# First batch in float32 through PV: probabilities scaled in place and turned by TensorE's one-pass float32 transpose

## The chip, the cores and the metric

The kernel runs on one core of one Trainium2 chip. The metric is device time in microseconds (us) of one execution; lower is better. Three runs of the kernel before gave 605.25, 607.4 and 608.04 us, median 607.4.

## What is computed

Causal attention over 4 batches, 12 heads, 448 positions and head size 64, and behind it a dense gated layer over all 1792 rows. The weights arrive as 64-bit floats.

```python
scores = (1.0 / np.sqrt(64)) * np.matmul(q, k.transpose(0, 1, 3, 2))
scores = np.where(mask, -1000000000.0, scores)          # mask: above the diagonal
scores = scores - np.max(scores, axis=-1, keepdims=True)
attn = np.exp(scores)
attn = attn / (np.sum(attn, axis=-1, keepdims=True) + 1e-09)
a = np.matmul(attn, v)                                  # [4, 12, 448, 64]
x = a.transpose(0, 2, 1, 3).reshape(1792, 768)
h = x @ w_in                                            # [768, 2048]
out = (h * (1.0 / (1.0 + np.exp(-1.702 * h)))) @ w_out  # [2048, 768]
```

## The kernel before

**Tiling.** The 448 positions of a batch are 7 chunks of 64. `cuts` makes two blocks of each batch: chunks 0 to 3 and chunks 4 to 6, so there are 8 blocks; n = 0 and n = 1 are batch 0. The 12 heads go in 6 pairs (u = 0 to 5, a "unit"); the two heads of a pair lie on the two halves of the 128 partitions. A chunk i looks at i + 1 chunks of keys, that is i // 2 + 1 tiles of 128 columns.

**Numbers.** Most products are float32 made of two float16 halves, high and low: `scaled` makes the high half (ScalarE or VectorE), `rest` the low half (VectorE), and three products (high-high, high-low, low-high) are added in PSUM. `halves` (L410) makes a product as two matmuls of 64 columns of the stationary operand. In batch 0 (`f32(b, u)`, L831) queries and keys stay float32 as they are: `turn` (L859) turns them by matmuls against an identity, and `scores32` multiplies in float32.

**A unit** (`unit`, L1174): scores into `ps_s`; `chunk` (L1079) subtracts the maximum and masks on VectorE (L1086) and takes the exponential on ScalarE (L1100), both in the float32 tiles `z`, of which there is one set for all units; GpSimd adds 1e-9 to the row sums (L1203); VectorE takes 1/sum (L1209). Then P = z/sum must be turned, so that the keys lie on the partitions. In block 0 (`pet=(0,)`) `p_turned` (L1129) builds a diagonal matrix of 1/sum (L1140, GpSimd or VectorE), multiplies z by it on TensorE in float32 into `ps_h`, and splits the result into `PT`, high and low. In all other blocks `p_pair` (L1112) splits z/sum into `p16`, high and low, and one DMA transpose (L1223) turns it into `PT`. `pv` (L1238) multiplies with V in three float16 products into `ps_v`, and every second unit splits the result into `xT`.

**V.** `v_batch` (L771) loads a whole batch's V into `vraw` in four loads, takes its largest norm (in batch 0 by the products of `gram` on TensorE, L610) and a scale from it; `v_pair` (L808) splits V for two units into `v16`.

**The dense layer.** `w_in_slice` (L633) loads, converts to float32 (`to_f32`: VectorE, and partly ScalarE) and splits one of 8 slices of w_in into `wib`; `w_out_load`, `w_out_scale` and `w_out_split` do the same for w_out, some of its raw data passing through `vraw`. `h_slice` (L1297) multiplies a block's `xT` with a slice into one of three `ps_h` buffers, and ScalarE and VectorE make the gate and the split `gT` from it; `out_tile` (L1350) multiplies with w_out and stores.

**Order.** Nothing runs by loop order: every step is given to `Ops.add` with its cost on each engine that may do it (the first named is preferred), its reads and writes, a priority and the time on the DMA engines. `Ops.order` tries 1500 orders on that model, with a model of TensorE's clock, and the best is issued: a fixed sequence for each engine's queue and for SP, which issues all DMAs.

## Time and profile before

| | |
|---|---|
| median of three runs | 607.4 us |
| profiled execution, its own time | 608.42 us |
| its span | 606.7 us |
| TensorE matmul (PE) busy | 567.6 us, 94% |
| VectorE (DVE) busy | 422.1 us, 70% |
| ScalarE (ACT) busy | 358.5 us, 59% |
| GpSimd (POOL) busy | 101.9 us, 17% |
| mean granted TensorE clock | 0.994 |

The span runs from the first to the last instruction. Busy shares are means over a kernel with different stages, so they are read by stretch of time. PEld is TensorE's loading of weights, which overlaps PE; SPq is SP's queue, which issues DMAs. A group of matmuls in the view in order of time carries about 0.2 us of modelled end, which the next group overlaps. "DMA" is the mean busy share of 16 DMA engines, "clock" the granted share of 2.4 GHz. In a row of a group, the numbers behind the bar are busy us, mean ns of one, and idle us before them with what ended it.

### The profile page before, as it was taken

Reading aid. Unit: us, or ns where it says so; the run is one execution under the profiler, and the core shown is the slowest. Engines: PE = TensorE matmul, PEld = TensorE weight load, DVE = VectorE, ACT = ScalarE, POOL = GpSimd, SP = SyncE. Lnnn points to the kernel's source line nnn. Section 1 sums busy time; section 2 is a strip of 40 time slices with the busy share of each in tenths; the row PEclk is TensorE's granted clock in tenths of the full one; section 3 lists DMA queues with packets and bytes.
Section 4 is the critical chain, followed back from the end, with each engine's and each line's share of the span. In section 5 each row is a group of like instructions: output and inputs, shape, how many; then the busy total and the mean of one; then the engine's idle time right before and its main releaser. Section 6 shows DMA issues by size and latency. Waiting matters only on the chain. (4 is left out here: it accounts for less than half of the span.)

```text
span 606.7 us, 22564 instructions
## 1 busy us (share of the span) xinstructions
PE 567.6 (94%) x9646; PEld 510.2 (84%) x9646; DVE 422.1 (70%) x1121; ACT 358.5 (59%) x826; POOL 101.9 (17%) x239
## 2 busy tenths in 40 slices
PE   4767798989999999999999999999999999999997
PEld 3555687876889899988988899998999999899986
DVE  3999999999978899977589869786686431202020
ACT  5779898998857767666566457675464321202120
POOL 2343330215410024110011223111000000000000
PEclk9999899999999999999999999999999999999999
DMA  8999579968688998998954998758662400000000
GB/s 278 228 311 296 178 230 315 237 141 149 123 178 162 162 165 144 166 168 163 171 99 85 167 176 144 144 99 139 96 122 58 90 14 16 1 28 3 28 27 28
DMA packets 217028, 83.84 MB, mean 138 GB/s; under 512 B 197728, under 2 KB 206688, under 8 KB 216928
## 3 DMA queue, kind: packets, MB, share of 16 engines
q1 hardware_dynamic: 216928, 82.40, 64.7%
q8 instruction: 75, 1.23, 0.8%
q14 instruction: 25, 0.20, 0.1%
HBM read 41.68 MB, written 5.51 MB: 78 GB/s over the span
## 5 line engine op out<-in xcount | busy, mean ns | idle before, releaser
L413 PE MATMUL ps_h<-xT,wib 128*64 128x192 f16 (+1 forms) x4608 | 247.1, 260 | 1.2 <-DVE gT L478 1.2
L1375 PE MATMUL ps_o<-wob,gT 128*64 128x384 f16 x2688 | 244.0, 326 | 1.6 <-DVE wob L478 1.4
L413 PEld LDWEIGHTS <-wib 128*64 128x64 f16 x4608 | 229.4, 110 | 7.2 <-issue 2.9
L1375 PEld LDWEIGHTS <-gT 128*64 128x64 f16 x2688 | 179.4, 110 | 31.9 <-issue 4.1
L1100 ACT ACTIVATE z<-z,cols 128x320 f32<-128x320 f32 (+6 forms) x168 | 84.0, 501 | 48.4 <-DVE cols L1086 47.3
L1337 DVE SCALAR_TENSOR_TENSOR ps_h<-t,ps_h 128x512 f32<-128x512 f32 (+1 forms) x64 | 40.1, 626 | 85.5 <-ACT t L1332 84.9
L1332 ACT ACTIVATE t<-ps_h,cols 128x512 f32<-128x512 f32 (+1 forms) x64 | 40.2, 629 | 73.6 <-PE ps_h L413 68.2
L478 DVE SCALAR_TENSOR_TENSOR p<-z,cols,p 128x384 f16<-128x384 f32 (+3 forms) x144 | 73.9, 541 | 3.3 <-ACT p L473 2.5
L1086 DVE CUSTOM_DVE_ANT_0 z<-ps_s,mask,cols 128x320 f32<-128x320 f32 (+6 forms) x126 | 56.7, 479 | 11.5 <-PE ps_s L1063 10.8
L1203 POOL TENSOR_SCALAR cols<-cols 128x2 f32<-128x2 f32 (+1 forms) x68 | 23.9, 352 | 195.4 <-ACT z L1100 184.1
L473 ACT ACTIVATE p<-z,cols 128x384 f16<-128x384 f32 (+3 forms) x82 | 44.6, 562 | 15.3 <-DVE cols L1209 8.2
L478 DVE SCALAR_TENSOR_TENSOR gT<-ps_h,gT 128x512 f16<-128x512 f32 (+1 forms) x64 | 39.4, 619 | 10.0 <-ACT gT L473 9.4
L1063 PE MATMUL ps_s<-kT,qT 128*64 128x64 f16 (+4 forms) x504 | 42.5, 273 | 1.8 <-DVE cols L1086 1.7
L1241 PE MATMUL ps_v<-PT,v 128*64 128x192 f16 (+3 forms) x864 | 41.3, 237 | 1.9 <-DVE xT L478 1.8
L1241 PEld LDWEIGHTS <-v 128*64 128x64 f16 x864 | 40.0, 110 | 3.6 <-issue 2.6
L473 ACT ACTIVATE gT<-ps_h 128x512 f16<-128x512 f32 (+1 forms) x54 | 29.4, 544 | 19.3 <-DVE ps_h L1337 19.0
L473 ACT ACTIVATE ob<-ps_o,cols 128x384 f32<-128x384 f32 x22 | 12.6, 573 | 37.6 <-PE ps_o L1375 37.6
L1100 ACT ACTIVATION_READ_ACCUMULATOR z<-z,cols 128x1 f32 x168 | 31.8, 189 | 0.0
L1063 PEld LDWEIGHTS <-qT 128*64 128x64 f16 x504 | 26.7, 110 | 5.5 <-issue 3.0
L1021 POOL TENSOR_SCALAR q<-q 128x512 f16<-128x512 f16 (+1 forms) x28 | 19.4, 694 | 54.5 <-ACT q L473 47.4
L475 DVE TENSOR_SCALAR p<-z,cols 128x256 f16<-128x256 f32 (+3 forms) x62 | 25.1, 423 | 3.7 <-DMA PT<-p 2.6
L473 ACT ACTIVATE wob<-wob 128x768 f32<-128x768 f32 (+1 forms) x20 | 22.1, 1104 | 7.7 <-DMA wob<-in_moe_w_in_dram 7.0
(95 smaller groups left out, 580.1 us busy)
## 6 DMA issues: line engine op xcount, KB each, us to landing
wob<-in_moe_w_in_dram SPq DMA_DIRECT2D x16, 768.0 KB, 6.9
wob<-in_moe_w_out_dram SPq DMA_DIRECT2D x9, 768.0 KB, 6.0
vraw<-in_moe_w_out_dram SPq DMA_DIRECT2D x7, 768.0 KB, 5.5
out_dram<-ob SPq DMA_DIRECT2D x28, 192.0 KB, 2.4
vraw<-in_v_dram SPq DMA_DIRECT2D x12, 384.0 KB, 5.1
kf<-in_k_dram SPq DMA_DIRECT2D x36, 112.0 KB, 3.5
qf<-in_q_dram SPq DMA_DIRECT2D x48, 64.0 KB, 2.8
qf<-in_q_dram SPq DMA_DIRECT2D x48, 48.0 KB, 2.8
```

Source lines behind the costliest of these rows:

```text
L413: nc.tensor.matmul(out[o : o + 64], lhsT[:, o : o + 64], rhs, start=start, stop=stop)
L473: nc.scalar.activation(out=dst, in_=src, func=AF.Copy, scale=sc)
L475: nc.vector.tensor_scalar(out=dst, in0=src, scalar1=sc, scalar2=None, op0=ALU.mult)
L478: nc.vector.scalar_tensor_tensor(out=dst, in0=src, scalar=sc, in1=hi, op0=ALU.mult, op1=ALU.subtract)
L1063: nc.tensor.matmul(ps[64 * j : 64 * j + 64], qt[:, g, i - c0, 64 * j : 64 * j + 64], kt[:, : i + 1, 64 * j : 64 * j + 64], start=(g == 0), ...
L1086: lambda e: nc.vector.tensor_tensor_reduce(out=z[:, :w], in0=ps, in1=mask[:, S - w :], scale=c, scalar=3.0e38, op0=ALU.add, op1=ALU.min, a ...
L1100: lambda e: nc.scalar.activation(out=z[:, :w], in_=z[:, :w], func=AF.Exp, bias=m, scale=-1.0, accum_out=l),
L1203: lambda e, ls=ls: by(e).tensor_scalar(out=ls, in0=ls, scalar1=1e-9, scalar2=2.0**-14, op0=ALU.add, op1=ALU.mult),
L1241: nc.tensor.matmul(ps[64 * j : 64 * j + 64, 64 * (first - c0) : w], vt[:, gv, J, j, :], PT[pi][:, at, gp, 64 * j : 64 * j + 64], start=(t ...
L1332: lambda e: nc.scalar.activation(out=th, in_=ph, func=AF.Tanh, scale=ts[:, sl : sl + 1]),
L1337: lambda e: nc.vector.scalar_tensor_tensor(out=ph, in0=th, scalar=1.0, in1=ph, op0=ALU.add, op1=ALU.mult),
L1375: nc.tensor.matmul(po[64 * j : 64 * j + 64, :OH], gT[:, f, gg, 64 * r : 64 * r + 64], wo_pair(f, gw, nh), start=(f == 0 and gg + gw == 0), ...
```

## The change

Batch 0 (blocks 0 and 1) is kept in float32 through PV.

- The probabilities z are multiplied by 1/sum in place; GpSimd is the first choice, ScalarE and VectorE are named too. TensorE then turns each tile with its transpose mode in float32, one instruction a tile, into `ps_h`, and one copy brings a group of tiles to `PT`, used as float32. This now holds for block 1 too, in place of `p_pair` and the DMA transpose.
- `pv` multiplies float32 V with float32 P, one product in place of three.
- V of batch 0 is loaded in 12 loads straight into the `v16` buffers as float32; nothing splits it. Its norm still sets a scale, which is now applied where `xT` is split.
- Block 1's turning uses `ps_h` buffer 2 only, and block 0's `h_slice` buffers 0 and 1.
- The planner's costs of TensorE's steps are changed, and it makes 600 rounds instead of 1500.

```diff
-    ROUNDS, STEPS, SPREAD = 1500, 6, (0.0, 0.5, 1.0, 2.0)
+    ROUNDS, STEPS, SPREAD = 600, 6, (0.0, 0.5, 1.0, 2.0)
...
-        add({"PE": len(blocks) * 0.1}, mm, keys, [ps_key], prio)
+        add({"PE": len(blocks) * 0.0585}, mm, keys, [ps_key], prio)
...
+    def v_first(prio):
+        st = bst[0]
+        sq, sq_key = col("sqv1", 2)
+        full = S // P
+        for u in range(0, NU, 2):
+            i = v16_r.next()
+            x = v16[i].rearrange("p g j h d -> p (g j h d)").bitcast(F32).rearrange("p (j h d) -> p j h d", j=NJ, d=D)
+            keys = [("v16", i, 0), ("v16", i, 1)]
+            add({"POOL": 0.5}, lambda e, x=x: nc.gpsimd.memset(x[S % P :, full], 0.0), [], keys[1:], -1e6)
+            src = v[0, 2 * u : 2 * u + 4]
+            for j in range(NJ):
+                r = min(P, S - j * P)
+                add(
+                    {"SP": Ops.LOAD},
+                    lambda e, x=x, src=src, j=j, r=r: nc.sync.dma_start(
+                        out=x[:r, j], in_=src[:, j * P : j * P + r].rearrange("h p d -> p h d")
+                    ),
+                    [], keys[: 1 if j == 0 else 2] if r == P else keys[1:], prio[u // 2], dma=0.81 * r / P,
+                )
+            for a in range(2):
+                st["v32", u + a] = x[:, :, 2 * a : 2 * a + 2], keys
+            gram(
+                x.rearrange("p j h d -> p j (h d)"), keys, ps_o[1], ("O", 1), u == 0, u == NU - 2, prio[-1]
+            )
+        gram_max(ps_o[1], ("O", 1), sq, sq_key, prio[-1])
+        v_scale(0, sq, sq_key, "O", prio[-1])
...
+    def flip_over(dst, src):
+        nc.tensor.matmul(dst, src, ident, start=True, stop=True, is_transpose=True)
...
-        add({"PE": 2 * (4 * r / 2.4 + 210) / 1e3}, mm, keys + ident_keys, [("T", h)], prio)
+        add({"PE": 2 * (4 * r / 2.4 + 5) / 1e3}, mm, keys + ident_keys, [("T", h)], prio)
...
-            add({"PE": (4 * o / 2.4 + 150 * len(run)) / 1e3}, scores32, [qt_key] + kt_keys, bank(sb), prio)
+            add({"PE": (4 * o / 2.4 + 6 * len(run)) / 1e3}, scores32, [qt_key] + kt_keys, bank(sb), prio)
...
+    def p_turned(n, run, pi, pp_i, where, rs, r_key, prio):
+        groups = [[(where[i, J], J, a, i) for J in range(i // 2 + 1)] for a, i in enumerate(run)]
+        if sum(len(x) for x in groups) <= 4:
+            groups = [[x for y in groups for x in y]]
+        for a, i in enumerate(run):
+            wp = (i // 2 + 1) * P
+            add(
+                {**pool(wp), **act(wp, ap=1), **dve(wp, ap=1, rate=0.521)},
+                lambda e, a=a, i=i: by_scale(e, z_of(i), rs[:, a : a + 1]),
+                [r_key], z_keys(i), prio,
+            )
+        for tiles in groups:
+            tiles = sorted(tiles)
+            p0, nt = tiles[0][0], len(tiles)
+            hb = ps_h_r.next() if n == 0 else 2
+            ps = ps_h[hb][:, : nt * P]
+
+            def mm(e, tiles=tiles, ps=ps, p0=p0):
+                for at, J, a, i in tiles:
+                    flip_over(ps[:, (at - p0) * P : (at - p0 + 1) * P], z_of(i)[:, J])
+
+            add(
+                {"PE": (nt * 60 + 2 * 93) / 1e3},
+                mm,
+                ident_keys + [k for i in {t[3] for t in tiles} for k in z_keys(i)], [("H", hb)], prio,
+            )
+            add(
+                {**act(nt * P, psum=True), **dve(nt * P)},
+                lambda e, ps=ps, p0=p0, nt=nt: scaled(
+                    e, p_f32(pi)[:, p0 : p0 + nt], ps.rearrange("p (a w) -> p a w", w=P), 1.0
+                ),
+                [("H", hb)], [("PT", pi, x) for x in range(p0, p0 + nt)], prio,
+            )
...
-            if n in TUNE["pet"]:
-                p_turned(run, pi, pp_i, where, rs, r_key, prio)
+            if f32(b, u):
+                p_turned(n, run, pi, pp_i, where, rs, r_key, prio)
                 continue
...
-            terms += [(J, first, slice(at[0], at[-1] + 1, step), gv, gp) for gv, gp in ((0, 0), (0, 1), (1, 0))]
+            pairs = ((0, 0),) if f32(b, u) else ((0, 0), (0, 1), (1, 0))
+            terms += [(J, first, slice(at[0], at[-1] + 1, step), gv, gp) for gv, gp in pairs]
...
-                        vt[:, gv, J, j, :],
-                        PT[pi][:, at, gp, 64 * j : 64 * j + 64],
+                        vt[:, J, j] if f32(b, u) else vt[:, gv, J, j, :],
+                        (p_f32(pi)[:, at] if f32(b, u) else PT[pi][:, at, gp])[:, :, 64 * j : 64 * j + 64],
...
+        sc, ap = (bst[b]["s_v"], 1) if f32(b, u) else (2.0**-14, 0)
...
-            lambda e: scaled("ACT", hi, ps_v[:, :, :w], 2.0**-14),
+            lambda e: scaled("ACT", hi, ps_v[:, :, :w], sc),
...
-        hb = ps_h_r.next()
+        hb = sl % 2 if n == 0 else ps_h_r.next()
...
-                    {"PE": 6 * (OH / 2.4 + 6) / 1e3},
+                    {"PE": 6 * (OH / 2.4 + 2.5) / 1e3},
...
-                v_batch(0, TUNE["v0"])
+                v_first([TUNE["v0"] + 10.0 * x for x in range(NU // 2)] + [TUNE["v0"] + 30.0])
```

## Rows read from the trace of the kernel before

**Rows 1.** Busy tenths in 40 equal slices of the span, from the page.

```profile
PE   4767798989999999999999999999999999999997
...
DVE  3999999999978899977589869786686431202020
```

**Rows 2.** Stretches: us; busy us (count) of PE PEld DVE ACT POOL; clock; DMA.

```profile
0.00:10.00 10.00, 2.59 (x14) 1.61 (x16) 1.74 (x4) 5.13 (x8) 4.32 (x20) 1.00 0.76 252
10.00:70.00 60.00, 42.48 (x690) 33.02 (x686) 57.82 (x139) 48.72 (x106) 22.11 (x40) 0.97 0.94 272
70.00:110.00 40.00, 36.07 (x600) 31.12 (x602) 39.22 (x79) 35.74 (x64) 7.05 (x13) 0.96 0.88 247
110.00:160.00 50.00, 47.07 (x728) 37.94 (x726) 49.12 (x112) 45.21 (x85) 14.58 (x31) 1.00 0.77 164
160.00:607.00 447.00, 439.36 (x7628) 406.48 (x7622) 274.19 (x792) 223.72 (x565) 53.83 (x136) 1.00 0.58 105
```

**Rows 3.** Matmuls by tile and line: ns min/median/max, first and last start us.

```profile
L413 PE MATMUL ps_h<-xT,wib x1116: 243/271/421, 70.9 to 199.0; 128*64 128x256 f16 x96, 128*64 128x192 f16 x90
...
L1375 PE MATMUL ps_o<-wob,gT x2688: 322/326/350, 121.0 to 602.1; 128*64 128x384 f16 x192
```

**Rows 4.** Stretches, instructions on PT alone: length, PE, DVE, ACT, clock, DMA.

```profile
0.00:70.00 70.00, 3.58 (x60) 5.79 (x11) 4.99 (x11) 0.98 0.91 269
70.00:120.00 50.00, 2.80 (x60) 0.69 (x1) 0.58 (x1) 0.97 0.89 247
```

**Rows 5.** The same for v: PE, PEld, DVE, ACT, clock, DMA.

```profile
0.00:70.00 70.00, 3.58 (x60) 3.08 (x60) 5.42 (x5) 1.15 (x1) 0.98 0.91 269
```

**Rows 6.** The same for p: PE, PEld, DVE, ACT, POOL, clock, DMA.

```profile
0.00:70.00 70.00, 10.39 (x144) 7.65 (x144) 0.42 (x1) 0.00 (x0) 9.16 (x11) 0.98 0.91 269
70.00:120.00 50.00, 0.00 (x0) 0.00 (x0) 6.11 (x9) 5.54 (x9) 0.00 (x0) 0.97 0.89 247
120.00:160.00 40.00, 0.00 (x0) 0.00 (x0) 5.55 (x9) 4.86 (x8) 0.00 (x0) 1.00 0.73 143
```

**Rows 7.** Instructions in order of time, PE: start us, us, what.

```profile
30.09 1.09 PE L413 MATMUL ps_h<-p,z 128*64 128x128 f32 x16 [0.67 <-POOL p L1140]
...
66.47 0.69 PE L1241 MATMUL ps_v<-PT,v 128*64 128x256 f16 x12 [0.49 <-DVE xT L478]
...
136.65 0.81 PE L413 MATMUL ps_s<-kT,qT 128*64 128x384 f32 x4
137.30 1.00 PE L1241 MATMUL ps_v<-PT,v 128*64 128x192 f16 x24
```

**Rows 8.** Groups of 0 to 120 us, then instructions in order of time.

```profile
L478 DVE SCALAR_TENSOR_TENSOR wib<-wob,cols,wib 128x1536 f16<-128x1536 f32 x8 | 15.3, 1916 | 0.4 <-ACT wib L473 0.3
...
L1140 POOL TENSOR_TENSOR p<-ident,cols 128x256 f32<-128x256 f32 x11 | 9.2, 833 | 7.9 <-DVE cols L1209 4.5 <-PE ps_o L867 3.4
...
22.07 0.61 POOL L1140 TENSOR_TENSOR p<-ident,cols 128x256 f32<-128x256 f32 x1 [2.39 <-DVE cols L1209]
...
22.76 0.19 POOL L1203 TENSOR_SCALAR cols<-cols 128x2 f32<-128x2 f32 x1
...
23.43 1.31 POOL L1140 TENSOR_TENSOR p<-ident,cols 128x256 f32<-128x256 f32 x1 [0.20 <-DVE cols L1209]
...
24.30 2.05 DVE L478 SCALAR_TENSOR_TENSOR wib<-wob,cols,wib 128x1536 f16<-128x1536 f32 x1
...
74.35 1.82 DVE L478 SCALAR_TENSOR_TENSOR wib<-wob,cols,wib 128x1536 f16<-128x1536 f32 x1 [0.34 <-ACT wib L473]
```

**Rows 9.** Instructions in order of time, SP's queue.

```profile
9.79 0.43 SPq L777 DMA_DIRECT2D vraw<-in_v_dram  x1
...
92.36 5.52 SPq L1223 DMA_TRANSPOSE PT<-p  x1
```

**Rows 10.** Two stretches of 5 us, columns as in rows 2.

```profile
55.00:60.00 5.00, 3.13 (x31) 2.07 (x33) 5.00 (x8) 4.96 (x14) 0.30 (x1) 0.77 0.72 207
70.00:75.00 5.00, 4.50 (x47) 4.42 (x49) 4.48 (x11) 4.12 (x5) 1.35 (x3) 0.66 0.40 145
```

More of the change, by code (lines that the diff above doesn't have):

```diff
@@ L783, in v_batch @@
         sq, sq_key = col("sqv1", 2)
-        if b == 0 and TUNE["gram_v"]:
-            x = vraw.rearrange("p j h d -> p j (h d)")
-            for j in range(NJ):
-                gram(
-                    x[:, j : j + 1], [("vraw", j, h) for h in range(2)], ps_o[1], ("O", 1), j == 0, j == NJ - 1, prio
-                )
-            gram_max(ps_o[1], ("O", 1), sq, sq_key, prio)
-        for j in range(2 * NJ if not (b == 0 and TUNE["gram_v"]) else 0):
+        for j in range(2 * NJ):
             square_sum(
@@ L796, in v_batch, with v_scale @@
             )
-        if not (b == 0 and TUNE["gram_v"]):
-            add(
-                dve(2 * NJ),
-                lambda e: nc.vector.tensor_reduce(out=sq, in_=sqv, axis=AX.X, op=ALU.max),
-                [(sqv_key, j) for j in range(2 * NJ)], [sq_key], prio,
-            )
-        amx, amx_key = all_max(sq, sq_key, "v", "S" if b else "O", prio)
+        add(
+            dve(2 * NJ),
+            lambda e: nc.vector.tensor_reduce(out=sq, in_=sqv, axis=AX.X, op=ALU.max),
+            [(sqv_key, j) for j in range(2 * NJ)], [sq_key], prio,
+        )
+        v_scale(b, sq, sq_key, "S", prio)
+    def v_scale(b, sq, sq_key, place, prio):
+        st = bst[b]
+        amx, amx_key = all_max(sq, sq_key, "v", place, prio)
         st["s_v"], st["s_v_key"] = col("s_v", 2)
@@ new lines, in p_turned @@
+    def p_turned(n, run, pi, pp_i, where, rs, r_key, prio):
[12 more added lines that the diff above has]
+            p0, nt = tiles[0][0], len(tiles)
+            assert [t[0] for t in tiles] == list(range(p0, p0 + nt)) and nt <= 4
+            hb = ps_h_r.next() if n == 0 else 2
[8 more added lines that the diff above has]
+            )
+            add(
+                {**act(nt * P, psum=True), **dve(nt * P)},
[3 more added lines that the diff above has]
+                [("H", hb)], [("PT", pi, x) for x in range(p0, p0 + nt)], prio,
+            )
@@ L1174, in unit, with by_scale, p_f32 @@
+    def by_scale(e, x, sc):
+        if e == "POOL":
+            nc.gpsimd.tensor_scalar(out=x, in0=x, scalar1=sc, scalar2=None, op0=ALU.mult)
+        else:
+            scaled(e, x, x, sc)
+    def p_f32(pi):
+        return PT[pi].rearrange("p a g w -> p (a g w)").bitcast(F32).rearrange("p (a w) -> p a w", w=P)
     def unit(n, u, prio):
@@ L1203, in unit @@
                 lambda e, ls=ls: by(e).tensor_scalar(
-                    out=ls, in0=ls, scalar1=1e-9, scalar2=2.0**-14, op0=ALU.add, op1=ALU.mult
+                    out=ls, in0=ls, scalar1=1e-9, scalar2=1.0 if f32(b, u) else 2.0**-14, op0=ALU.add, op1=ALU.mult
                 ),
@@ L1218, in unit @@
         ne = len(places)
-        all_keys = [("PT", pi, x) for x in range(4)]
-        if n not in TUNE["pet"]:
+        all_keys = [("PT", pi, x) for x in range(NPT)]
+        if not f32(b, u):
           add(
@@ L1249, in unit @@
         add(
-            {"PE": sum((64 * (c1 - t[1]) / 2.4 + 5) for t in terms) / 1e3}, pv, v_keys + all_keys, [("PV", vb)], prio,
+            {"PE": sum(((4 if f32(b, u) else 1) * 64 * (c1 - t[1]) / 2.4 + 3) for t in terms) / 1e3}, pv, v_keys + all_keys, [("PV", vb)], prio,
         )
@@ L1257, in unit @@
         keys = [[("xT", x, u - a, g) for a in range(2)] for g in range(2)]
[L1258 to L1266 removed]
+        sc, ap = (bst[b]["s_v"], 1) if f32(b, u) else (2.0**-14, 0)
+        sc_keys = [bst[b]["s_v_key"]] * ap
+        add(
+            act(2 * w, psum=True, ap=ap),
+            lambda e: scaled("ACT", hi, ps_v[:, :, :w], sc),
+            pv_keys + sc_keys, keys[0], prio,
+        )
+        add(
+            dve(2 * w, ap=ap),
+            lambda e: rest(lo, ps_v[:, :, :w], sc, hi),
+            pv_keys + sc_keys + keys[0], keys[1], prio,
         )
@@ L1301, in h_slice @@
         x = n % 2
-        hb = ps_h_r.next()
+        hb = sl % 2 if n == 0 else ps_h_r.next()
         ph = ps_h[hb].rearrange("p (t w) -> p t w", t=2)[:, :, :w]
@@ L1319, in h_slice @@
                 add(
-                    {"PE": 3 * half * (w / 2.4 + 2.5) / 1e3},
+                    {"PE": 3 * half * (w / 2.4 + 2.6) / 1e3},
                     mm,
@@ L1438, in keys_values @@
                 k_pair(b, u, at(n, u) - TUNE["dk"])
[L1439 to L1441 removed]
+            if b:
+                v_pair(b, u, at(n, u) - TUNE["dv"])
     for n, (b, c0, c1) in enumerate(blocks):
```

57 lines of the change are left out of this document (3 added, 54 removed).

## The prediction

> **What bounds the kernel now.** I read the 40 slices of the page first. TensorE (PE) is at 9 from about slice 12 on and between 4 and 9 before it, while VectorE (DVE) is at 9 from slice 1 [rows 1]. So whatever can be won lies ahead of about 160 us. The busy times by stretch say how much [rows 2]: PE is idle for 7.4 us of the first 10, for 17.5 us between 10 and 70, for 3.9 us between 70 and 110, for 2.9 us between 110 and 160, and for 7.6 us in the 447 us behind that. The sum is 39.4 us. DVE is idle for 2.2 us between 10 and 70 and for 1.7 us between 70 and 160. The kernel before is thus a stretch that DVE limits, followed by one that PE limits; I call them stage A (to 70 us), stage B (70 to 160 us) and the rest. Stage A ends where the first big matmuls start: `h_slice` of block 0 at 70.9 us [rows 3]. The output matmuls run from 121.0 to 602.1 us, and what comes behind their last one (4.6 us to the end of the span at 606.7) is the last eviction and store, which the change leaves alone.
>
> The profiled execution took 608.42 us for a span of 606.7; the median of the runs is 607.4. I take differences against the profiled span and set them on the median.
>
> **What leaves VectorE.** (1) In block 0 the turned probabilities were split into a high and a low half; the low half was a DVE instruction. They are 11 before 70 us and one behind it, 5.79 and 0.69 us [rows 4]. (2) V of batch 0 is no longer split: 5 DVE instructions, 5.42 us, all before 70 us [rows 5]. (3) One of the 12 diagonals ran on DVE, 0.42 us; in block 1 the split of P leaves, 18 instructions, 6.11 us between 70 and 120 and 5.55 us between 120 and 160 [rows 6]. Stage A loses 5.79 + 5.42 + 0.42 = 11.6 us of DVE work, stage B 0.69 + 6.11 + 5.55 = 12.4 us.
>
> **What ScalarE gains or loses.** One V split (1.15 us) leaves stage A [rows 5]. In block 0 the copy out of PSUM stays. In block 1 a copy out of PSUM takes the place of the high half of P. The nearest rows are 11 copies of 256 or 512 columns in 4.99 us, 0.45 us each [rows 4], against 9 high halves of 384 or 512 columns in 5.54 us, 0.62 us each [rows 6]; by the column these are nearly equal. I take 1 us less in stage A and nothing in stage B.
>
> **What TensorE gains or loses.** In block 0 a unit's six probability tiles were turned by float32 matmuls against a diagonal. A group of four tiles is 16 matmuls in 1.09 us, of which about 0.2 us is the modelled tail that every group carries, so 0.22 us a tile and 36 x 0.22 = 7.9 us [rows 7]. A one-pass transpose does not occur in this trace. Its bounds are the same 0.22 us (four passes) and a quarter of it, 0.055 us; the change names one pass, so I take 0.06. Block 0 then pays 2.2 us, and block 1 pays 60 tiles x 0.06 = 3.6 us that it did not have (at the other end 13 us, and block 0 would save nothing). PV becomes one float32 product instead of three of 16 bits. A float32 product of 384 columns in two column halves takes 0.81 us with its tail, 0.61 without [rows 7]; block 0's PV has 384 columns a unit and takes 0.69 with its tail now, block 1's has 640 and takes 1.00. So 0.61 + 0.2 against 0.69, and 1.02 + 0.2 against 1.00: 0.12 and 0.22 us a unit, and with 4/3 of the columns' time as the other estimate 0.16 and 0.27. I take 1 us for block 0 and 1.6 us for block 1. Stage A: -7.9 + 2.2 + 1.0 = -4.7 us; stage B: +3.6 + 1.6 = +5.2 us; in all +0.5 us.
>
> **What GpSimd gains.** The diagonals (11 of 0.833 us, 9.2 us) leave [rows 8]. A scaling in place of 128 to 512 float32 columns is not in the trace. From 0.19 us for 2 columns and 0.61 for 256 [rows 8] I estimate 1.67 ns a column: 0.40, 0.61, 0.83 and 1.04 us. Block 0 has 2 x 0.40 + 2 x 0.61 a unit, 12.1 us; block 1 has 2 x 0.83 + 1.04 a unit, 16.2 us. GpSimd is 37% busy between 10 and 70 [rows 2], so it has room. But its queue is in order: behind a scaling stand the additions to the row sums (L1203) and the exponent steps of the weights' scales (L447, L454), and who waits for those is DVE's reciprocal and the split of a w_in slice. A scaling also holds the single set of z tiles longer, and the next unit's masking waits for it; the diagonal, 0.61 us for a pair of chunks, stood at the same place in the chain, so the chain of block 0 grows by 0.2 to 0.6 us a pair against a unit period of 10 us (six units in the 60 us), and I cost it at nothing while PE and DVE have other work.
>
> The scaling also meets DVE at the memory. A diagonal takes 0.61 us beside DVE work out of PSUM, but 1.31 us where DVE is in a split out of SBUF, and DVE's next split then takes 2.05 us instead of 1.82 [rows 8]. The eight w_in splits take 1.916 us on average, 0.8 us above eight of 1.82; I put about 1 us of DVE's time down to 9.2 us of diagonals, 0.11 a microsecond. For 28.3 us of scalings that is 3 us, 2 more than now; the bounds are 0 and every microsecond, 28. I take 1 us in stage A and 2 in stage B. The Trainium skill ("SBUF — State Buffer", section "SBUF: two separate sides") says that the pair of ports shared by VectorE and GpSimd is an exclusive lock and the loser blocks for the whole instruction. The rows agree that there is a wait, but DVE's was 0.23 us of an overlap of 0.44, so part of an instruction is not held.
>
> **Queues.** Six transposes of P by DMA leave SP's queue in block 1; the one at 92.36 us held the queue for 5.5 us, with w_out loads behind it [rows 9]. Against that V of batch 0 comes in 12 loads instead of 4, eight more issues of 0.43 us on SP [rows 9], some 3.4 us in stage A; the V data are the same. V goes straight to its place, so nothing reads `vraw` before the w_out loads use it. Block 1's turning has one PSUM buffer of its own and block 0's `h_slice` two instead of three: a slice is 72 matmuls, and its drain four instructions out of PSUM of the size of [rows 4] (0.45 us), which run while PE fills the other buffer or does block 1's attention. I cost both at nothing; if that cover is gone, PE waits up to one drain, some 2 us, a slice, 16 us in all, and DVE's relief is what keeps the drain short.
>
> **The sum.** Stage A: DVE and ScalarE were busy for 57.8 and 48.7 us of the 60 between 10 and 70 [rows 2]. With 11.6 - 1 us less on DVE and 1 less on ScalarE it is 94.9 us for both; the order may hand work to either. At the shares they reach now at best (0.96 and 0.90) that is 51 us, so stage A ends 9 us earlier. PE then needs 42.5 - 4.7 = 37.8 us of these 51 and does not bind. Stage B: PE's own work grows by 5.2 us, and its idle 6.8 us is what can be taken back. DVE has 12.4 - 2 us less to do in 90 and the DMA transposes are gone, so I take 5 of the 6.8; the bounds are 0 and 6.8. Net +0.2 us. The rest stays. Sum: -9 + 0.2 = -8.8 us, 607.4 - 8.8 = **598.6 us**. The planner's costs for PE are also changed, and it makes fewer rounds; the whole order changes with that. No row prices it: I take 0 and allow some 5 us to both sides, so this case alone spans 593 to 604.5. At the four-pass end of the transposes stage B gets 13.2 - 3.6 = 9.6 us more and the time is 608, which sets the high end of the range.
>
> **Rivals.** *Better filled* (chance 0.15): DVE and PE now need about the same time ahead of 160 us (127 and 129 us), and an order that knows it fills PE. Its idle time falls from 39.4 to the 7.4 at the start, some 4.3 at the end and about 8 more: 607.4 - 19.7 + 0.5 = 588.2 us. Against it: with one full engine PE still idled 2.9 us in every 10 here until 70 us.
>
> *Transfers hold stage A* (0.09): the DMA share between 10 and 70 is 0.94 [rows 2] and no byte of stage A goes. Then stage A does not shrink, and the time is 607.4 + 0.2 = 607.6 us, no change. Against it: the share is 0.72 between 55 and 60 and the rate 207 GB/s against 272 over the stage [rows 2, 10], so there are holes.
>
> *The scaling is not done by GpSimd* (0.04): the planner may give it to ScalarE or DVE. At 0.45 us each, as the copies of [rows 4], block 0's 24 are about 11 us for the two engines in stage A, nearly all of what was taken: about 606 us; DVE took one diagonal in 12 here [rows 6].
>
> *Slower: DVE pays for every scaling* (0.06): if every microsecond of GpSimd's scalings stops DVE, stage A gets 12.1 us for the 11.6 it lost and stage B 16.2 for 12.4. Stage A then stays (+0.5), and stage B takes the 5.2 us of new PE work on top with nothing taken back: 607.4 + 0.5 + 5.2 = 613 us. It decides from about half a microsecond for each: then stage A gives (12.6 - 6.0) / 1.86 = 3.5 us and stage B, with DVE's relief down to 4.3 us and some 2 us of idle taken back, costs 3.2. The rows give 0.11.
>
> *Slower: the clock* (0.04): the granted clock was 0.77 between 55 and 60 us and 0.66 between 70 and 75, but 0.97 over 10 to 70 with PE 71% busy [rows 2, 10]. If the transposes thin PE out and it is granted 1.2 GHz, its 37.8 us of stage A double at most, to 76 us instead of 51: 25 us more, 624 us. It decides from 13 us of PE work at half clock; below that DVE sets the stage anyway. In the shorter stage PE is busier (0.74) than now (0.71), which speaks against it. The Trainium skill ("TensorE: Matmul & The Clock Gate", "Part 4: PE-mode transpose") says that transposes do not count as busy for the clock as matmuls do; without the 2.2 us of them the share would be 0.70, as now, so it changes little here. No row shows a transpose.
>
> **How the numbers follow.** The forecast has 0.62. The range of 588 to 608 takes in the first four cases but about half of *better filled*, and leaves the slower two out: some 0.18. A measurement of this kernel can tell about 0.5% from no change, here 604.4 and 610.4. Faster: 0.59 of the forecast, 0.15 and a little of the third rival, 0.75. Same: 0.03 of the forecast, the transfers and most of the third, 0.15. Slower: 0.10, the last two.
>
> **What would show it.** The first `h_slice` matmul at about 62 us instead of 70.9; no DVE lines on PT, v and p of batch 0; about 24 us less DVE work ahead of 160 us; PE idle of about 30 us instead of 39; turning of four tiles in about 0.25 us without the tail; scalings on GpSimd of 0.4 to 1.0 us, stretched where DVE splits out of SBUF. I am wrong if the first `h_slice` matmul stays near 70 us, if the granted clock falls through stage A, or if new idle stretches of PE open behind 160 us, where a different order may wait for DMA.

## The result: slower by 1.5%, and the profile after

The changed kernel takes 616.75 us (median; 614.67 to 617.84) where the kernel before takes 607.72 beside it: 1.0147 times as long (95% interval 1.0099 to 1.0195). The forecast was 598.6 with a range to 608, so sign and size were wrong, by 18 us. The profiled execution took 617.84 us for a span of 616.1.

The page of the changed kernel, its engines and its 40 slices, against [rows 1]:

```profile
PE 577.7 (94%) x9526; PEld 510.3 (83%) x9526; DVE 414.4 (67%) x1107; ACT 347.5 (56%) x818; POOL 126.2 (20%) x257
...
PE   2777979899999999999999999999999999999997
...
DVE  3788987799989689977767858897788422202200
...
POOL 2362454532712010411101113121010000000000
PEclk9979979899999999999999999999999999999999
```

DVE stood at 9 nearly without a break from slice 1 to 11; now it rarely does. That is the relief I wanted, and PE did not fill the room. GpSimd (POOL) stands at 4 to 7 in six of the first eleven slices, in three before.

The stretches of the changed kernel (columns as in [rows 2]):

```profile
10.00:70.00 60.00, 43.63 (x580) 32.99 (x580) 49.10 (x133) 46.58 (x107) 22.04 (x34) 0.91 0.90 268
70.00:110.00 40.00, 34.30 (x513) 28.17 (x512) 34.26 (x64) 32.96 (x54) 21.46 (x24) 0.91 0.60 184
110.00:160.00 50.00, 47.93 (x716) 38.74 (x716) 45.24 (x97) 39.83 (x77) 21.58 (x33) 0.97 0.61 149
```

Between 10 and 160 us DVE is idle for 21.4 us (3.8 before), GpSimd is busy for 65 us (44 before), the transfers fall from 0.88 to 0.60 in the third row, and the granted clock from 0.97 to 0.91, 0.96 to 0.91 and 1.00 to 0.97. DVE is no longer the bound ahead of 160 us, and PE is idle as long as before. The page's span less PE's busy time gives its idle time for each kernel, and that account carries all that follows:

| kernel | span | PE busy | PE idle |
|---|---|---|---|
| before | 606.7 | 567.6 | 39.1 |
| forecast for the change | 597.9 | 568.1 | 29.8 |
| after | 616.1 | 577.7 | 38.4 |
| after, scaling left out (e2) | 604.4 | 572.7 | 31.7 |
| after, GpSimd's scalings done by DVE (e1) | 608.1 | 575.1 | 33.0 |

So the forecast failed twice: the idle time that was to go is still there, and PE has 10.1 us more of busy time where I had +0.5.

Where PE's idle time comes from: the waits of the changed kernel that involve the scaling (L1191, in place on z) and the transposes (L881); us in total, times, longest.

```profile
PEld ps_h L881 <- POOL z L1191: 15.2, 14, 2.4
...
PE ps_h L881 <- POOL z L1191: 10.6, 8, 2.2
POOL z L1191 <- DVE cols L1233: 10.2, 16, 2.1
...
DVE z L1110 <- PE ps_h L881: 5.4, 6, 1.3
```

In the kernel before, the wait at the same place was for GpSimd's diagonal:

```profile
PE ps_h L413 <- POOL p L1140: 3.3, 6, 1.0
```

It ended 3.3 us of PE's idle time; now 10.6 us of it ends with GpSimd's scaling. The last line of the changed kernel's waits is the next link: DVE's masking of the following unit waits until the transposes have read the single set of z tiles. This is the chain of which the prediction says "I cost it at nothing while PE and DVE have other work".

The scalings by themselves, in order of time (start, us, count, idle before):

```profile
20.26 0.61 POOL L1191 TENSOR_SCALAR z<-z,cols 128x128 f32<-128x128 f32 x1 [0.48 <-DVE cols L1233]
...
162.56 1.56 POOL L1191 TENSOR_SCALAR z<-z,cols 128x512 f32<-128x512 f32 x1 [0.36 <-DVE cols L1233]
166.00 1.24 POOL L1191 TENSOR_SCALAR z<-z,cols 128x384 f32<-128x384 f32 x1 [0.74 <-DVE cols L1233]
```

These are the shortest of their sizes: 0.61, 1.24 and 1.56 us for 128, 384 and 512 columns, or (1.56 - 0.61) / 384 = 2.5 ns a column and 0.29 us beside it. The forecast had 1.67 ns: 0.40, 0.83 and 1.04. And most are longer, as the same scalings show in groups (0 to 170 us; busy us, mean ns; idle before and what ended it). The four of 256 columns take 1.39 us on average.

```profile
L1191 POOL TENSOR_SCALAR z<-z,cols 128x384 f32<-128x384 f32 x10 | 16.7, 1679 | 5.4 <-DVE cols L437 2.8 <-DVE cols L1233 2.5
...
L1191 POOL TENSOR_SCALAR z<-z,cols 128x512 f32<-128x512 f32 x5 | 9.0, 1791 | 2.3 <-DVE cols L1233 2.3
...
L1191 POOL TENSOR_SCALAR z<-z,cols 128x128 f32<-128x128 f32 x6 | 7.5, 1248 | 3.2 <-DVE cols L1233 3.1
```

One chain of the changed kernel, beside DVE's split of a w_in slice, shows what a long one does. The view names a group of scalings by the size of its first:

```profile
32.95 1.00 DVE L472 TENSOR_SCALAR wib<-wob,cols 128x1536 f16<-128x1536 f32 x1
33.03 4.31 POOL L1191 TENSOR_SCALAR z<-z,cols 128x128 f32<-128x128 f32 x3 [0.20 <-DVE cols L1233]
...
34.13 1.84 DVE L475 SCALAR_TENSOR_TENSOR wib<-wob,cols,wib 128x1536 f16<-128x1536 f32 x1
...
34.65 0.48 PE L881 MATMUL ps_h<-ident,z 128*128 128x128 f32 x1 [0.89 <-POOL z L1191]
...
36.50 0.47 PE L881 MATMUL ps_h<-ident,z 128*128 128x128 f32 x1 [1.37 <-POOL z L1191]
...
37.01 0.29 DVE L1110 CUSTOM_DVE_ANT_0 z<-ps_s,mask 128x128 f32<-128x128 f32 x1 [1.03 <-PE ps_h L881]
```

The three scalings of the 4.31 us are two of 128 columns and one of 256, as the same stretch (32.9 to 37.4 us) shows by size:

```profile
L1191 POOL TENSOR_SCALAR z<-z,cols 128x128 f32<-128x128 f32 x2 | 3.4, 1713 | 0.2 <-DVE cols L1233 0.2
L1191 POOL TENSOR_SCALAR z<-z,cols 128x256 f32<-128x256 f32 x1 | 0.9, 917 | 0.0
```

The two of 128 columns, 0.61 us undisturbed, take 1.71 us each while DVE works in SBUF from 32.95 to 35.97. The one of 256 columns comes behind that, beside DVE's masking out of PSUM (37.01), and takes 0.92 us, which is what 2.5 ns a column and 0.29 us give. PE, in order, takes one tile, waits, takes one tile, waits; then DVE waits for PE.

DVE's own splits did not grow: eight of the kind of 34.13 take 1.817 us on average, 1.916 before [rows 8] and 1.813 in a run without any scaling (e2 below). So in these rows GpSimd is held up beside DVE, and DVE hardly beside GpSimd; elsewhere DVE lost a little too (a split of w_out at 160.74 us, begun during a scaling, took 1.33 us where its kind takes 1.04 on average). The Trainium skill ("SBUF — State Buffer", section "SBUF: two separate sides") says that VectorE and GpSimd share a pair of ports under an exclusive lock and the loser blocks. The rows fit that in part, with GpSimd as the loser: the split at 78.88 us began during a scaling and took its usual 1.82 us. No run here measured the contest by itself. The prediction looked at what it costs the winner.

In groups over the whole span the changed kernel has (line, engine, form, count; busy us, mean ns; idle before and what ended it):

```profile
L1266 PE MATMUL ps_v<-PT,v 128*64 128x192 f16 (+7 forms) x792 | 44.7, 256 | 0.9 <-DVE xT L475 0.6
...
L1191 POOL TENSOR_SCALAR z<-z,cols 128x384 f32<-128x384 f32 (+3 forms) x25 | 38.7, 1552 | 13.2 <-DVE cols L1233 10.2
...
L881 PE MATMUL ps_h<-ident,z 128*128 128x128 f32 x96 | 18.4, 305 | 11.7 <-POOL z L1191 10.6
```

25 of the 42 scalings are on GpSimd and take 38.7 us; all 42 were forecast at 28.3. The 96 one-pass transposes take 18.4 us, where 5.8 was forecast. In a row they are shorter than their mean says, but not 0.06 us. PE's transposes in groups of four, two and six tiles, in order of time:

```profile
22.95 0.66 PE L881 MATMUL ps_h<-ident,z 128*128 128x128 f32 x4
...
42.70 0.44 PE L881 MATMUL ps_h<-ident,z 128*128 128x128 f32 x2 [0.75 <-POOL z L1191]
...
46.55 0.87 PE L881 MATMUL ps_h<-ident,z 128*128 128x128 f32 x6 [0.95 <-POOL z L1191]
```

Each further tile adds (0.87 - 0.44) / 4 = 0.107 us: 96 x 0.107 = 10.3 us, and the other 8 us are the tails of the groups, which the sum left out, before and after. Like for like, without tails, it is 10.3 us against the 5.8 of the forecast.

### The profile page after: what moved, and what is told of

The parts are those of the page before. It is cut to its first block, busy times and chain, and to the rows that moved or that the text cites. A ratio compares the mean times of both kernels' runs of the same rounds, so it can differ in the third digit from the quotient of the medians.

```text
span 616.1 us, 22317 instructions
## 1 busy us (share of the span) xinstructions
PE 577.7 (94%) x9526; PEld 510.3 (83%) x9526; DVE 414.4 (67%) x1107; ACT 347.5 (56%) x818; POOL 126.2 (20%) x257
## 3 DMA queue, kind: packets, MB, share of 16 engines
q1 hardware_dynamic: 201504, 78.47, 61.1%
## 4 chain that ended last, share of the span: by engine, by line
PE 73%; DVE 12%; POOL 6%; DMA 4%; issue 2%; ACT 2%; SPq 0%; DVEq 0%; ACTq 0%; POOLq 0%
PE ps_o L1402 31%; PE ps_h L410 28%; PE ps_v L1266 4%; POOL z L1191 4%; PE ps_s L1087 4%; DVE z L1110 2%; DMA PT<-p 2%; PE ps_h L881 2%; PE ps_s L410 1%; PE ps_o L891 1%; DVE p L475 1%; DMA q<-in_k_dram 1%; PE ps_o L410 1%; POOL cols L1304 1%; DVE wob L597 1%
## 5 line engine op out<-in xcount | busy, mean ns | idle before, releaser
L410 PE MATMUL ps_h<-xT,wib 128*64 128x256 f16 (+1 forms) x4608 | 247.2, 261 | 1.1 <-DVE gT L475 0.9
L1124 ACT ACTIVATE z<-z,cols 128x320 f32<-128x320 f32 (+5 forms) x168 | 84.0, 501 | 69.8 <-DVE cols L1110 66.9
L1110 DVE CUSTOM_DVE_ANT_0 z<-ps_s,mask,cols 128x128 f32<-128x128 f32 (+6 forms) x126 | 57.4, 478 | 24.7 <-PE ps_s L1087 24.2
L475 DVE SCALAR_TENSOR_TENSOR p<-z,cols,p 128x128 f16<-128x128 f32 (+3 forms) x126 | 62.1, 524 | 2.4 <-ACT p L470 1.6
L470 ACT ACTIVATE p<-z,cols 128x256 f16<-128x256 f32 (+3 forms) x72 | 38.4, 546 | 16.3 <-DVE cols L1233 13.7
L1266 PE MATMUL ps_v<-PT,v 128*64 128x192 f16 (+7 forms) x792 | 44.7, 256 | 0.9 <-DVE xT L475 0.6
L1087 PE MATMUL ps_s<-kT,qT 128*64 128x192 f16 (+4 forms) x504 | 42.0, 273 | 1.2 <-DVE cols L1110 1.2
L1191 POOL TENSOR_SCALAR z<-z,cols 128x384 f32<-128x384 f32 (+3 forms) x25 | 38.7, 1552 | 13.2 <-DVE cols L1233 10.2
L410 PE MATMUL ps_s<-kT,qT 128*64 128x320 f32 (+6 forms) x168 | 26.1, 424 | 4.8 <-ACT kT L470 1.9
L881 PE MATMUL ps_h<-ident,z 128*128 128x128 f32 x96 | 18.4, 305 | 11.7 <-POOL z L1191 10.6
```

The lines of the kernel that those rows point to most:

```text
L410: nc.tensor.matmul(out[o : o + 64], lhsT[:, o : o + 64], rhs, start=start, stop=stop)
L470: nc.scalar.activation(out=dst, in_=src, func=AF.Copy, scale=sc)
L475: nc.vector.scalar_tensor_tensor(out=dst, in0=src, scalar=sc, in1=hi, op0=ALU.mult, op1=ALU.subtract)
L881: nc.tensor.matmul(dst, src, ident, start=True, stop=True, is_transpose=True)
L1087: nc.tensor.matmul(ps[64 * j : 64 * j + 64], qt[:, g, i - c0, 64 * j : 64 * j + 64], kt[:, : i + 1, 64 * j : 64 * j + 64], start=(g == 0), ...
L1110: lambda e: nc.vector.tensor_tensor_reduce(out=z[:, :w], in0=ps, in1=mask[:, S - w :], scale=c, scalar=3.0e38, op0=ALU.add, op1=ALU.min, a ...
```

## The experiments

The theory after the result: GpSimd's scaling, too slow and in the chain ahead of PE, costs the time. Its rivals: the changed order of the planner (its prices and rounds are part of the diff), the price of the transposes, and the granted clock, which may fall with them. "After's order" means that the planner runs as in the changed kernel and only what is emitted is edited; `scalings` holds the numbers of the 42 scalings.

**e1: after's order, GpSimd's 25 scalings done by VectorE.**

```diff
...
-            ops.ops[i][1](e)
+            ops.ops[i][1]("DVE" if i in scalings and e == "POOL" else e)
```

> The changed kernel with its order kept; only the 25 scalings that GpSimd had are done by VectorE. Theory G (TensorE's queue waits for GpSimd's scalings, which took 1.25 to 1.79 us on average in place of the 0.4 to 1.04 that I had put in, and the clock falls in these waits): VectorE does one of 128 to 256 columns in 0.30 to 0.34 us (its own ten in the changed kernel), so the waits for the scaling (10.6 us on PE, 15.2 on its weight loads) mostly go and the time comes to 603 to 610 us. Theory T (TensorE's own work grew: a transpose costs 0.11 us a tile and not 0.06, and it does not hold the clock): the transposes stay, 613 to 618 us. Theory O (the order made with other prices and fewer rounds is worse, whatever runs in it): the order stays, 613 to 618 us.

Measured: 608.36 us (606.65 to 610.29), 1.001 of before [0.999, 1.0031]. The same step as the chain above, in this kernel:

```profile
32.77 1.00 DVE L473 TENSOR_SCALAR z<-z,cols 128x128 f32<-128x128 f32 x4
33.11 0.69 PE L882 MATMUL ps_h<-ident,z 128*128 128x128 f32 x2 [0.54 <-DVE z L473]
```

All four scalings of the step take 1.00 us on DVE, where GpSimd's three took 4.31. Moving 25 instructions to another engine, with nothing else changed, gives back 8.4 of the 9.0 us. That the loss is GpSimd's scaling in its place is shown, not argued. Of the 8.0 us between the two profiled spans, 5.4 are PE's idle time and 2.6 its busy time, for the same matmuls; e2 says more on that.

**e2: after's order, no scaling at all.** All 42 are left out, so the probabilities are not normalised.

```diff
...
-            ops.ops[i][1](e)
+            if i not in scalings:
+                ops.ops[i][1](e)
```

> The changed kernel with its order kept; the scaling by 1/sum is left out altogether, so the probabilities of batch 0 are not normalised. It takes away GpSimd's 38.7 us of scalings and VectorE's and ScalarE's share. Theory G: 600 to 608 us, the waits of TensorE for the scaling are gone, and with them the half clock. Theories T and O: 613 to 618 us, as transposes and order stay.

Measured: 605.2 us (603.07 to 606.6), 0.9953 [0.9934, 0.9973]. The first stretches (columns as in [rows 2]) and the first `h_slice` matmul (ns min/median/max, first to last start, forms):

```profile
10.00:70.00 60.00, 46.61 (x650) 35.91 (x652) 50.39 (x131) 47.74 (x107) 12.95 (x30) 0.91 0.91 270
70.00:110.00 40.00, 35.83 (x574) 29.34 (x572) 37.25 (x72) 35.14 (x64) 6.48 (x13) 1.00 0.69 227
...
L411 PE MATMUL ps_h<-xT,wib x4608: 246/258/298, 62.8 to 580.1; 128*64 128x256 f16 x96, 128*64 128x192 f16 x96
```

This is the forecast with its scaling made free: the first `h_slice` matmul starts at 62.8 (forecast 62, after 66.5, before 70.9), and PE is idle for 31.7 us (forecast 29.8). Scaling as the changed kernel does it thus costs it 11.6 us, and scaling on DVE 3.2 (e1 less e2).

Not all of that is waiting. Of the 11.7 us between the two profiled spans, 6.7 are PE's idle time and 5.0 its busy time, for the same matmuls in the same order. The clock holds most of the 5.0: it was 0.91, 0.91 and 0.97 in the three stretches from 10 to 160 us in the changed kernel, and is 0.91, 1.00 and 1.00 here. PE's busy time of each stretch times the missing share is 8.5 us there and 4.2 here, 4.3 us less (an estimate from these rows). So the scaling costs PE twice: it waits, and more of its matmuls run at 1.2 GHz.

What is left between 605.2 and 598.6 is mostly PE's own work, +5.1 us instead of +0.5. The turning, without tails, is 96 x 0.107 = 10.3 us against the 7.9 of the kernel before, +2.4 where the sum had -2.1; with the +2.6 that the sum had for PV this gives +5.0, an estimate that meets the +5.1. (The groups of the view carry tails that other groups overlap, and do not add up to PE's busy time: the turning's goes from 10.4 to 18.0 us, PV's from 41.3 to 43.2.)

**e3: the kernel before with the changed kernel's prices for PE and 600 rounds.** Nothing of the computation changes.

```diff
-    ROUNDS, STEPS, SPREAD = 1500, 6, (0.0, 0.5, 1.0, 2.0)
+    ROUNDS, STEPS, SPREAD = 600, 6, (0.0, 0.5, 1.0, 2.0)
...
-        add({"PE": len(blocks) * 0.1}, mm, keys, [ps_key], prio)
+        add({"PE": len(blocks) * 0.0585}, mm, keys, [ps_key], prio)
...
-            {"PE": nt * (4 * P / 2.4 + 150) / 1e3},
+            {"PE": nt * (4 * P / 2.4 + 6) / 1e3},
...
```

> The kernel before with nothing but the planner's changed TensorE prices and 600 rounds in place of 1500 (the price of its own float32 turning is mended in the same way, from 150 to 6 ns a tile). Theory O: this alone loses most of the 9 us, 613 to 618 us. Theories G and T: within 4 us of the kernel before, 604 to 612 us.

Measured: 612.84 us (612.59 to 616.31), 1.0103 [1.0056, 1.015]. PE is busy for 567.7 us as before, and idle for 43.5 instead of 39.1. The time lies just between the two ranges expected. Prices and rounds, and with them the order alone, cost 5 us. e1 shows that this order's cost isn't simply carried into the changed kernel: with the planner as changed and a quick scaling it stands level with before.

**e7 and e8: after and before with another seed of the planner.**

```diff
-SEED = 2
+SEED = 3
```

> The changed kernel with another start of the planner's random search, nothing else. It shows how much of a difference an order alone makes. Theory O (the order found is a draw, worth several us): anywhere from 609 to 622 us. Theory G: within 3 us of the changed kernel, 614 to 620 us.

Measured: 616.39 us (615.45 to 616.82), 1.0125 [1.0093, 1.0158]. 32 scalings are now on GpSimd (46.5 us), and PE's wait for them is 14.4 us. Two orders lose the same, so the loss isn't one unlucky order.

> The kernel before with another start of the planner's random search, nothing else. Theory O: the order of the kernel before is a good draw that the change gave up, 610 to 616 us, as with the changed prices and 600 rounds (612.8). If only the changed prices made that order worse: 605 to 609 us.

Measured: 611.07 us (608.44 to 611.66), 1.0046 [1.0025, 1.0066]. Another draw costs the kernel before 3 us, about half of the 5 us of e3. Together with e3 this suggests that the order of before is a good draw, and that an edit which makes the planner draw again may start with a few us against it. My +/- 5 us had the size; with 0 as its middle it did not see on which side the kernel at hand stands.

**e4: after, planned with the measured prices** of the GpSimd scaling (with 0.5 us added) and the transpose.

```diff
-                {**pool(wp), **act(wp, ap=1), **dve(wp, ap=1, rate=0.521)},
+                {"POOL": (2.5 * wp + 290) / 1e3 + 0.5, **act(wp, ap=1), **dve(wp, ap=1, rate=0.521)},
...
-                {"PE": (nt * 60 + 2 * 93) / 1e3},
+                {"PE": nt * 107 / 1e3},
```

> The changed kernel planned anew with two prices as its trace shows them: a scaling on GpSimd 2.5 ns a column + 0.29 us, and 0.5 us more for what it waits for VectorE; a transpose 0.107 us a tile. Theory G, with the false price as its root: the planner gives scalings to other engines or leaves them time, PE's waits for them fall, 602 to 610 us. If GpSimd's place in the chain is what costs, whatever the price says, or under T: 611 to 618 us. Under O it may fall anywhere within some 5 us of 617.

Measured: 612.01 us (608.49 to 615.16), 1.0078 [1.0051, 1.0104]. The planner still gives GpSimd 23 scalings (32.3 us); PE's wait for them falls from 10.6 to 4.3 us, but the granted clock over 10 to 70 us is 0.80. That is 4.7 us better than the changed kernel, and outside the 602 to 610 of a false price as the root. As another draw alone is worth 3 us (e8), how much of the 4.7 the right price made isn't shown.

**e5: after with diagonals again.** Batch 0 keeps its float32 PV, but the scaling goes into a diagonal on GpSimd and PE turns with four-pass matmuls, in both blocks, as the kernel before did in block 0.

```diff
...
-                lambda e, a=a, i=i: by_scale(e, z_of(i), rs[:, a : a + 1]),
...
+            lambda e: by(e).tensor_tensor(
+                out=diag,
+                in0=ident.unsqueeze(1).to_broadcast([P, ln, P]),
+                in1=rs.unsqueeze(2).to_broadcast([P, ln, P]),
+                op=ALU.mult,
+            ),
...
-                    flip_over(ps[:, (at - p0) * P : (at - p0 + 1) * P], z_of(i)[:, J])
+                    halves(ps[:, (at - p0) * P : (at - p0 + 1) * P], z_of(i)[:, J], diag[:, a], True, True)
...
```

> The changed kernel with one part undone and planned anew: the probabilities of batch 0 are turned as the kernel before did it in block 0, by four-pass float32 products with a diagonal of 1/sum that GpSimd (or VectorE) builds, and nothing is scaled in place; float32 stays through PV. Theory G: GpSimd's step is back at 0.6 to 0.85 us a pair of chunks, so PE's waits for GpSimd fall to the 3 to 4 us of the kernel before and the time comes to 608 to 615 us, although the turning costs PE 96 x 0.22 = 21 us in place of 10. Theory T (TensorE's own work decides): 10 us more PE work, 620 us or more.

Measured: 616.43 us (616.1 to 617.12), 1.013 [1.0098, 1.0161], no better, and between the two ranges expected. PE's longest waits, in the order of the view:

```profile
PE ps_o L891 <- DMA q<-in_k_dram: 11.0, 6, 7.0
PE ps_h L410 <- POOL p L1166: 7.8, 5, 3.7
```

19 diagonals take 16.7 us of GpSimd where 25 scalings took 38.7, and PE still waits 7.8 us for them, and 11.0 us for k. This kernel was planned anew, so an order of its own is mixed in, and the run is inconclusive: it doesn't separate the diagonal from the scaling.

**e6: after's order, each tile turned by four-pass matmuls** instead of transpose mode.

```diff
-        nc.tensor.matmul(dst, src, ident, start=True, stop=True, is_transpose=True)
+        halves(dst, src, ident, True, True)
```

> The changed kernel with its order kept; each tile is turned by an ordinary float32 product with the identity (two halves of 64 columns, four passes) in place of the transpose mode. At 0.22 against 0.107 us a tile it adds 96 x 0.11 = 10.8 us of PE work. If the turning is on the path of PE: 622 to 628 us. If it hides in PE's waits for GpSimd: 616 to 620 us. If it is the transpose mode that lets the clock fall (0.50 between 30 and 35 us, with PE busy 2.3 of 5 us just before), the granted clock stays at 1.0 there and some 5 us come back; if it is the idle time, the clock falls there as before.

Measured: 616.23 us (614.71 to 617.28), 1.0131 [1.0091, 1.017], the same as after. The turning itself, as a group over the whole span:

```profile
L410 PE MATMUL ps_h<-ident,z 128*64 128x128 f32 x384 | 29.2, 291 | 11.5 <-POOL z L1191 10.5 <-DVE cols L437 0.8 <-DVE z L472 0.2
```

It takes 29.2 us instead of 18.4, and PE in all 577.1 instead of 577.7. Part of the reason is in the granted clock (the column after the five engines). First the changed kernel, then e6, the same stretches:

```profile
30.00:35.00 5.00, 2.75 (x17) 1.59 (x17) 4.99 (x9) 5.00 (x9) 3.68 (x3) 0.50 0.86 244
35.00:40.00 5.00, 3.56 (x23) 2.56 (x23) 2.39 (x7) 1.72 (x7) 2.53 (x3) 0.54 0.87 241
...
85.00:90.00 5.00, 5.00 (x44) 3.96 (x44) 3.92 (x5) 4.40 (x6) 0.98 (x3) 0.50 0.86 296
```

```profile
30.00:35.00 5.00, 1.76 (x20) 1.11 (x20) 4.99 (x9) 5.00 (x9) 3.78 (x3) 0.85 0.80 232
35.00:40.00 5.00, 3.85 (x38) 3.60 (x36) 2.38 (x7) 1.70 (x7) 2.44 (x3) 0.50 0.80 230
...
85.00:90.00 5.00, 4.49 (x58) 4.30 (x59) 3.91 (x4) 3.51 (x4) 1.88 (x4) 0.69 0.92 270
```

A clock of 0.50 is 1.2 GHz throughout the stretch. In the changed kernel PE had stood waiting, for scalings and for other things, with a few transposes between, before it got half clock for 30 to 35 and for 85 to 90 us. With four-pass turning the clock is 0.85 and 0.69 in these two places and 1.00 instead of 0.66 in 110 to 115 us, but no better in 35 to 40. What that is worth on the same work, 36 matmuls of one `h_slice` on PE, first in the changed kernel, then in e6 (start, us):

```profile
84.61 1.12 PE L881 MATMUL ps_h<-ident,z 128*128 128x128 f32 x4 [2.21 <-POOL z L1191]
85.66 4.05 PE L410 MATMUL ps_h<-xT,wib 128*64 128x256 f16 x36
```

```profile
85.51 1.98 PE L410 MATMUL ps_h<-ident,z 128*64 128x128 f32 x16 [1.89 <-POOL z L1191]
87.27 2.57 PE L410 MATMUL ps_h<-xT,wib 128*64 128x256 f16 x36
```

The four-pass turning of four tiles takes 0.86 us more, and the matmuls behind it 1.48 us less. Over the three stretches from 10 to 160 us the clock is 0.94, 0.96 and 1.00 where it was 0.91, 0.91 and 0.97; times PE's busy time that is some 4.5 us (an estimate), not the whole of the 10.8 us that the turning adds. The two profiled executions may also overstate it: they are the slowest of the changed kernel's (617.84 us) and the fastest of e6's (614.71).

The Trainium skill ("TensorE: Matmul & The Clock Gate", "Part 4: PE-mode transpose") says that transposes don't count as busy for the clock as matmuls do. These rows fit that, but do not show it: the four-pass form also keeps PE busy for twice as long a tile. The next run speaks against transposes as what decides the clock here.

**e11: e1 with four-pass turning.** Both edits above together.

```diff
-        nc.tensor.matmul(dst, src, ident, start=True, stop=True, is_transpose=True)
+        halves(dst, src, ident, True, True)
...
+            ops.ops[i][1]("DVE" if i in scalings and e == "POOL" else e)
```

> The changed kernel with its order kept, scalings by VectorE, and each tile turned by a four-pass float32 product with the identity in place of the transpose mode. Against the same with the transpose mode (608.4 us). The transposes add 10.8 us of PE work; if the transpose mode lets the clock fall, as the four-pass run with GpSimd's scalings showed (PE busy 577.1 against 577.7 us with 10.8 us more work), it comes out within 4 us of 608.4. If the clock there fell for the waits for GpSimd alone, which are gone here: 613 to 619 us.

Measured: 609.46 us (608.85 to 612.44), 1.0023 [1.0005, 1.0042], with 29.3 us of turning against 18.2. e1 stood at 1.001 [0.999, 1.0031] of before, so the two differ by about 0.8 us, and their intervals overlap. The first stretch of e1, then of e11 (columns as in [rows 2]):

```profile
10.00:70.00 60.00, 46.15 (x630) 34.91 (x630) 53.18 (x149) 47.74 (x109) 12.36 (x29) 0.91 0.92 270
```

```profile
10.00:70.00 60.00, 46.98 (x719) 39.66 (x721) 52.41 (x147) 47.00 (x108) 11.32 (x27) 0.91 0.92 270
```

The clock is 0.91, 0.96 and 1.00 from 10 to 160 us in both: with DVE's scalings the form of the turning doesn't change it. PE is busy for 580.0 instead of 575.1 us and idle for 30.7 instead of 33.0, so most of the added turning is hidden by tails and waits. The price that I took wrong (0.107 for 0.06 us a tile) was not what decided.

**e9, e10 and e12: planned with the scaling on VectorE or ScalarE.** e9 offers no GpSimd for it and has the measured transpose price; e10 is e9 with the old PE prices and 1500 rounds; e12 is e9 with seed 3.

```diff
...
-                {**pool(wp), **act(wp, ap=1), **dve(wp, ap=1, rate=0.521)},
+                {**dve(wp, ap=1, rate=0.521), **act(wp, ap=1)},
...
-                {"PE": (nt * 60 + 2 * 93) / 1e3},
+                {"PE": nt * 107 / 1e3},
```

> The changed kernel planned anew with the scaling offered to VectorE first and ScalarE second, not to GpSimd, and a transpose priced at its measured 0.107 us a tile. With the order kept, VectorE's scaling gave 608.4 us. If a plan that knows who scales does better than that: 603 to 607 us. If the draw of an order decides: 605 to 613 us.

Measured: 606.99 us (604.52 to 610.03), 0.9972 of before [0.9946, 0.9999], PE idle 605.5 - 574.9 = 30.6 us. Its first stretches (columns as in [rows 2]) and first `h_slice` matmul (columns as in e2):

```profile
10.00:70.00 60.00, 48.06 (x692) 36.30 (x692) 55.04 (x152) 50.92 (x114) 16.73 (x30) 1.00 0.93 273
...
L410 PE MATMUL ps_h<-xT,wib x4608: 246/259/422, 61.1 to 576.3; 128*64 128x256 f16 x96, 128*64 128x192 f16 x96
```

The best complete version: stage A ends 9.8 us earlier than before, at full clock. It is still only 0.3% better, since PE has 574.9 - 567.6 = 7.3 us more to do.

> As the run before (scaling on VectorE or ScalarE, planned, transpose at 0.107 us a tile), with all other TensorE prices and the 1500 rounds of the kernel before. If the changed prices are what costs some 5 us, as in the kernel before with changed prices (612.8): 600 to 605 us, below the run before by 3 or more. If orders are draws, it lies within 5 us of it to either side.

Measured: 610.68 us (609.12 to 613.01), 1.003 [1.0008, 1.0051]. The old prices and more rounds are no better here, so e3's loss can't be put down to worse prices or fewer rounds as such.

> As the first of these runs (scaling on VectorE or ScalarE, planned), with another start of the planner's search. If orders are draws of some 5 us: between 603 and 613 us, and not the time of the first. If scaling off GpSimd decides: within 3 us of the first, and below the 616.4 us that this start of the search gave with GpSimd.

Measured: 608.7 us (606.38 to 610.2), 1.0004 [0.9982, 1.0026], 1.7 us above e9. The gain of e9 over before is of the size of a draw.

## Why the prediction was wrong, point by point

**The step that failed: "I cost it at nothing".** The scaling stands between DVE's reciprocal and PE's transposes, in place on the only set of z tiles, ahead of PE's in-order queue. I compared it with the diagonal at the same place, let the chain grow by 0.2 to 0.6 us a pair, and hid that behind other work. Measured: 25 scalings of 1.55 us on average, 10.6 us of PE's idle time, and 11.6 us of the time as against no scaling (e2), 8.4 against scaling on DVE (e1); by the estimate at e2 some 4 of the 11.6 are not waits but matmuls at the lower clock. These 11.6 us and the 6.6 between e2 and the forecast are the whole miss of 18.2, and of the 6.6 PE's own work is 4.6.

**The price behind it.** I drew a line through 2 and 256 columns of other GpSimd instructions and called GpSimd "37% busy, so it has room". The slope was 2.5 ns a column, not 1.67, and the mean, with what DVE's work in SBUF cost GpSimd, was 1.25 to 1.79 us by size. My bounds were for DVE's loss; I gave none for GpSimd's own, though [rows 8] held it: 0.61 us against 1.31 for the same diagonal.

**The rival "DVE pays for every scaling" (613 us, 0.06)** had the sign and nearly the time, but not the mechanism: DVE's w_in splits are no longer than before, and DVE is idle for 21 us. GpSimd paid, and through the chain PE did.

**The rival "the clock" (624 us, 0.04)** happened in part: 0.91 over 10 to 110 us, and by the estimate at e2 some 4 us of the loss. It supposed that the transposes thin PE out, and I had written that their rule "changes little here". e1 and e11 bear that out: 0.91, 0.96 and 1.00 with either form. The changed kernel and e6 differ in clock, but not in time. As a cause it is second to the chain: it fell after PE had waited, and e1 has 0.91 over the first 60 us as well and stands at 608.

**The rival "transfers hold stage A"** is refuted: with a DMA share of 0.90 to 0.93 between 10 and 70 us, stage A ended at 66.5 us, 62.8 without scaling and 61.1 in e9. **"The scaling is not by GpSimd" (606 us)** came near in number, e1 608.4 and e9 607.0, but by luck: it let DVE's and ScalarE's scalings eat up stage A's relief. The relief stayed (first `h_slice` at 64.3 us in e1, 61.1 in e9), and PE's own work, +7.5 and +7.3 us, took the gain. I had it as what might befall; it was the better kernel.

**What held.** DVE bounds stage A, and the relief is real: e2's first `h_slice` and idle time are within 1 and 2 us of the forecast. Behind 160 us PE stays the bound. PV costs +1.9 to +3.4 us, where I had 2.6. **What was mis-sized:** PE's turning, -2.1 us by my sum and +2.4 by the measured 0.107 us a tile. Smaller slips moved little: PE stands at 9 from the tenth slice on, not the twelfth [rows 1]; DVE's best share is 0.98, between 70 and 110 us, and not 0.96 [rows 2], half a microsecond of stage A; and 598.6 +/- 5 is 593.6 to 603.6, not 593 to 604.5.

**The planner, 0 +/- 5 us:** e3 and e8 put the draws of before at +5 and +3, e9, e10 and e12 span 607.0 to 610.7 for one computation. Which of prices, rounds and chance makes an order good isn't settled by these runs; only that an order is worth some 3 to 5 us here. How much of after's 9 us a luckier order would spare is open too; e4, planned with the prices as measured, still lost 5.
